# Splitting the second-to-last V load 1/4 and 3/4 around the last K load, with five tiny reads of x in mid-run

## The chip, the cores and the metric

The kernel runs on one core of a Trainium2 chip. The metric is device time in microseconds (us), median of several executions; lower is better. Beside it stands one execution taken by the hardware profiler, with a record of each instruction, each DMA packet and each landing of a load.

Five engines matter here, and each runs its own instructions in program order: PE (TensorE, matmuls; PEld is its weight load), DVE (VectorE), ACT (ScalarE), POOL (GpSimd) and SP (SyncE), which here only issues DMAs. A DMA issued by SP is cut into packets and spread over the core's 16 DMA engines. The load has landed when all 16 have reported.

## The reference

A gated mix of two branches for a single token. Nearly all of the work is branch A: attention of 16 query heads over a cache of 8 key/value heads, 65536 positions and head size 256, in bfloat16.

```python
q = (x @ wq)                                   # 16 heads of 256
k = repeat(k_cache, 2); v = repeat(v_cache, 2) # 8 heads in the cache, 2 query heads for each
p = softmax(einsum("bhqd,bhkd->bhqk", q, k) / 16)
a = einsum("bhqk,bhkd->bhqd", p, v).reshape(1, 1, 4096) @ wo
b = mixer MLP of layernorm(x)                  # w1 1 x 1792, w2 1792 x 1
out = g * a + (1 - g) * b                      # g = sigmoid(sum(x * gate_w))
```

K and V are 8 x 65536 x 256 elements of 2 bytes each, 268 MB apiece. They are read once, and there are two query rows per key head, so the kernel is mostly the reading of 537 MB.

## The kernel before

**Blocks.** The cache is walked in 32 blocks (n = 0 to 31, L = 31 is the last), four per key head. A block is 16384 positions; partition p holds 128 consecutive positions of it, so a block's K, like its V, is 128 partitions x 128 rows x 256 elements, 8.4 MB. K goes into two tiles, kn0 (rows 0 to 63 of each partition) and kn1 (rows 64 to 127); V goes into one tile, vt, of 128 rows. There is one buffer of each, no second set.

**Work in a block.** `score_block(n)` (lines 352 to 364) takes K through 32 quarters (8 groups i of 16 rows, 4 quarters each). A quarter is four PE transposes into PSUM (line 329) and one DVE copy to SBUF (line 334). Each complete group is followed by eight score matmuls (line 343) that accumulate in `sc_ps`. The first 16 quarters read kn0, the other 16 read kn1. `softmax(n)` (line 380) takes the maximum, exponentials and the transposed weights `pT`. `pv(n, ip)` for ip = 0 to 3 (line 366) multiplies the weights with 32 rows of vt each: ip 0 needs rows 0 to 31, ip 1 rows 32 to 63, and so on; it is 16 matmuls (line 370). `accumulate` (line 416) adds the product to the running sum `acc`.

**Order.** `seq` ties every instruction to the one before it on its engine, so the order on each engine is the order of the text. All K and V loads are issued by SP. For most blocks SP issues after the scores of block n: V(n), then the two halves of K(n+1). A load waits until its tile has been read: V(n) for the products of block n-1, K(n+1) into kn0 for the first 16 quarters of block n, into kn1 for the other 16.

**The end.** For block L-1 the order (lines 510 to 514) is: rows 0 to 63 of V(L-1), K(L) into kn0, K(L) into kn1, rows 64 to 127 of V(L-1). The products of block L-1 are put off: two of the four stand within the scores of block L, as hooks at quarters 8 and 14 (line 501), and two stand after the softmax of block L (lines 531 and 532). V(L) isn't loaded into vt but into the two K tiles, in six pieces of 64, 32, 16, 8, 4 and 4 rows (`load_v_last`, line 121): the first into kn0, the other five into kn1. The products of block L (line 552) are another form: 128 rows, two matmuls each, V as the weights, 64 rows from kn0, then the collection of the earlier blocks' sum (`collect`, line 440), then 64 rows from kn1. A short epilogue (lines 560 to 572) scales, projects, copies and stores the output.

**Starting loads.** wq, x and the small vectors are loaded at the start, the small ones from ACT's queue; wo is loaded once in block 0.

Of the kernel before, what the change touches and what calls it, by code (L numbers as in the profile page):

```python
# [9 lines left out]
BF16 = mybir.dt.bfloat16  # L10
# [10 lines left out]
VP = BLK // 128  # L21
KP = VP // 2
NJ = 16
NI = VP // NJ
# [4 lines left out]
def kernel(  # L29
# [15 lines left out]
    nc = tc.nc  # L45
# [12 lines left out]
    def seq(ins):  # L58
        e = ins.ins.engine
        if e in last:  # L60
            tc.add_manual_dep(
                ins.ins,
                last[e],
                mybir.DependencyInfo(
                    mybir.DependencyClass.NoSync, mybir.DependencyReason.DATA
                ),
                reason="program order",
            )
        last[e] = ins.ins.name
        return ins  # L70

    const = ctx.enter_context(tc.tile_pool(name="const", bufs=1))
# [29 lines left out]
    def rows(cache, n):  # L102
        g, b = divmod(n, NB)
        return cache[0, g, b * BLK:(b + 1) * BLK, :].rearrange("(p j) d -> p j d", j=VP)

    def load_k(n, h, pieces=((0, KP),)):
        for j0, j1 in pieces:
            seq(nc.sync.dma_start(
                out=k_tiles[h][:, j0:j1, :],
                in_=rows(A_k_cache, n)[:, h * KP + j0:h * KP + j1, :],  # L110
            ))

    def load_v(n, j0=0, j1=VP):
        seq(nc.sync.dma_start(out=vt[:, j0:j1, :], in_=rows(A_v_cache, n)[:, j0:j1, :]))

    def pairs(ap):
        return ap.rearrange("p (i j) d -> p i j d", i=2)
# [3 lines left out]
    def load_v_last(n):  # L121
        for j0, j1 in LAST:
            seq(nc.sync.dma_start(
                out=k_tiles[j0 // KP][:, j0 % KP:(j1 - 1) % KP + 1, :],
                in_=rows(A_v_cache, n)[:, j0:j1, :],
            ))
# [4 lines left out]
        out=wq_t[:, :], in_=A_wq[DM:D, :].rearrange("r (h n) -> (r h) n", h=2)  # L131
    ))
    with nc.allow_non_contiguous_dma(reason="short rows"):
# [16 lines left out]
        out=val[:], in_=rowsel[:, :, :, 0:NI], op=ALU.add, axis=AXIS.XY  # L150
    ))
    fst = const.tile([128, 2, REP], FP32)
    for e in range(2):
        seq(nc.vector.tensor_reduce(
            out=fst[:, e, :], in_=rowsel[:, :, :, e:e + 1], op=ALU.add, axis=AXIS.XY
# [3 lines left out]
        out=par[:], in_=ident_f[:].rearrange("p (a r) -> p r a", r=REP), op=ALU.add, axis=AXIS.X  # L159
# [3 lines left out]
        out=nval[:], in0=val[:], scalar1=-scale, scalar2=None, op0=ALU.mult  # L163
# [7 lines left out]
        out=same[:], in_=val[:].unsqueeze(1).to_broadcast([128, 64, REP])  # L171
# [10 lines left out]
        out=xrr[:], in_=xr[:, DM:D].unsqueeze(2).to_broadcast([1, D - DM, 2])  # L182
    ))
    x_col = hd_ps[:, 40:44]
    for k in range(3):
# [13 lines left out]
        out=xtm[:], in0=par[:], scalar1=x_col[:, 3:4], scalar2=None, op0=ALU.mult  # L199
# [17 lines left out]
        out=veps[:], in0=mv[:, 1:2], scalar1=1e-5, scalar2=None, op0=ALU.add  # L217
# [5 lines left out]
    for _ in range(2):  # L223
# [3 lines left out]
            out=ntmp[:], in0=ntmp[:], scalar1=-0.5, scalar2=1.5, op0=ALU.mult, op1=ALU.add  # L227
# [3 lines left out]
        out=h_bc[:], in0=xf[:], scalar1=mv[:, 0:1], scalar2=rstd[:, 0:1],  # L231
        op0=ALU.subtract, op1=ALU.mult,
    ))
    for b in range(NF):
        seq(nc.scalar.activation(
            out=gel[:, b, :], in_=h_bc[:], func=ACT.Gelu_apprx_tanh,
# [4 lines left out]
    for h in range(HQ):  # L241
# [19 lines left out]
        out=qpad[:, :, :, 0, 0:REP],  # L261
        in_=q_ps.rearrange("p (c g r) -> p c g r", c=2, r=REP),
    ))
    for i in range(1, NI):
        seq(nc.vector.tensor_copy(
            out=qpad[:, :, :, i, i * REP:(i + 1) * REP], in_=qpad[:, :, :, 0, 0:REP]
# [58 lines left out]
    def transposes(i, quarter):  # L325
        tp = tps[state["t"] % 4]
        state["t"] += 1
        for jj in range(4):
            seq(nc.tensor.transpose(  # L329
                tp[:, jj * 128:(jj + 1) * 128],  # L330
                k_tiles[i // 4][:, i % 4 * NJ + quarter * 4 + jj, :].bitcast(FP32),
                ident_f[:, :],
            ))
        seq(nc.vector.tensor_copy(  # L334
            out=kT_tiles[i % 2][:, quarter * 4:(quarter + 1) * 4, :, :].rearrange(
                "p j n c -> p (j n c)"
            ),
            in_=tp[:, :].bitcast(BF16),
        ))

    def scores(g, i, c):
        for a in range(4):
            seq(nc.tensor.matmul(  # L343
                sc_ps[32 * a:32 * (a + 1), :],
                lhsT=qpad[:, c, g, i, :],
                rhs=kT_tiles[i % 2][:, :, 32 * a:32 * (a + 1), c],
                start=(i == 0 and c == 0),
                stop=(i == NI - 1 and c == 1),
                tile_position=(0, 32 * a),
            ))  # L350

    def score_block(n, hooks={}):
        due = []
        for t, (i, quarter) in enumerate((i, q) for i in range(NI) for q in range(4)):
            transposes(i, quarter)
            if due and due[0][0] <= t:
                scores(n // NB, *due.pop(0)[1])
            if quarter == 3:
                due.append((t + 2, (i, 0)))
                due.append((t + 3, (i, 1)))  # L360
            if t in hooks:
                hooks[t]()
        while due:
            scores(n // NB, *due.pop(0)[1])

    def pv(n, ip):
        pT = pT_tiles[n % 2]
        for jj in range(NJ):
            grp = jj % 4
            seq(nc.tensor.matmul(  # L370
                pv_ps[32 * grp:32 * grp + 2 * REP, :, :],
                lhsT=pT[:, 32 * jj + 2 * REP * ip:32 * jj + 2 * REP * (ip + 1)],
                rhs=pairs(vt[:, 32 * ip:32 * (ip + 1), :])[:, :, jj, :],
                start=(ip == 0 and jj < 4),
                stop=(ip == NI // 2 - 1 and jj >= NJ - 4),
                tile_position=(0, 32 * grp),
            ))
# [38 lines left out]
    def accumulate(n):  # L416
        if n % NB > 0:
            seq(nc.vector.scalar_tensor_tensor(  # L418
                out=acc[:], in0=acc[:], scalar=al_tiles[n % 2][:, 0:1], in1=pv_ps[:, :, :],
                op0=ALU.mult, op1=ALU.add,  # L420
            ))
        else:
            seq(nc.vector.tensor_copy(out=acc[:], in_=pv_ps[:, :, :]))  # L423
# [43 lines left out]
    L = NBLK - 1  # L467

    def products(n):
        for ip in range(NI // 2):  # L470
            pv(n, ip)
        accumulate(n)
# [14 lines left out]
    def last_wo():  # L487
        for r in range(REP):
            for c in range(2):
# [2 lines left out]
                    in_=wo_sb[:, HQ - REP + r, c, :].rearrange("p (m k) -> p k m", k=NCOL),  # L492
                ))

    for n in range(NBLK):
        if n == 0:
            score_block(n, {8: gate_sum, 20: mixer_tail})
        elif n < L:
            score_block(n, {5: gate_column, 16: last_wo} if n == 1 else {})
        else:  # L500
            score_block(n, {4: result_base, 8: lambda: pv(L - 1, 0), 14: lambda: pv(L - 1, 1)})
        if n < L - 1:
            load_v(n)
            load_k(n + 1, 0)
            load_k(n + 1, 1)
            if n == 0:
                seq(nc.sync.dma_start(
                    out=wo_sb[:], in_=A_wo.rearrange("(h p c) n -> p h c n", p=128, c=2)
                ))
        elif n == L - 1:  # L510
            load_v(n, 0, KP)
            load_k(L, 0)
            load_k(L, 1)
            load_v(n, KP, VP)
        else:
            load_v_last(L)
        softmax(n)
        if n == L:
            seq(nc.vector.tensor_scalar(
                out=esc[:], in0=fst[:], scalar1=al_tiles[L % 2][:, 0:1], scalar2=None, op0=ALU.mult  # L520
            ))
            seq(nc.vector.tensor_scalar(
                out=lsv[:], in0=val[:], scalar1=lsum[:, 0:1], scalar2=None, op0=ALU.mult
            ))
            f_ps = tps[0][:, 0:NCOL]
            for k in range(NCOL):
                seq(nc.tensor.matmul(  # L527
                    f_ps[:, k:k + 1], lhsT=base[0:1, k, :],
                    rhs=ones_f[0:1, 0:1], start=(k == 0), stop=False, skip_group_check=True,
                ))  # L530
            pv(n - 1, 2)
            pv(n - 1, 3)
            seq(nc.tensor.matmul(
                hd_ps[:, 456:456 + REP], lhsT=ones_f[:, :], rhs=lsv[:, :], start=True, stop=True
            ))
            accumulate(n - 1)
            seq(nc.vector.reciprocal(out=rdv[:], in_=hd_ps[:, 456:456 + REP]))
            seq(nc.vector.tensor_scalar(
                out=rdv[:], in0=rdv[:], scalar1=gcol[:, 0:1], scalar2=None, op0=ALU.mult
            ))  # L540
        if n < L - 1:
            if n % NB == NB - 1:
                denominators()
            products(n)
            if n % NB == NB - 1:
                head_end(n // NB)


    for j in range(VP):
        i, jj = divmod(j, NJ)  # L550
# [52 lines left out]
```

## Time and profile before

| | |
|---|---|
| Time, median of 3 runs | 1286.46 us (1286.38 to 1286.53) |
| The profiled execution, its own time | 1285.52 us |
| Its span, first to last instruction | 1283.7 us |
| Granted TensorE clock, mean | 0.862 of full speed |
| PE busy | 975.9 us (76%) |
| DVE busy | 756.1 us (59%) |
| ACT busy | 44.9 us (3%) |
| DMA moved | 545.5 MB, mean 425 GB/s |
| Packets under 512 B | 2260 of 17838 |
| K loads of a half block | 63 of 4096 KB, median 26.8 us from issue to landing |
| V loads of a block | 30 of 8192 KB, median 33.6 us from issue to landing |

The shares of busy time are averages over the whole run, in which most of the 32 blocks look alike and the last two don't. The change lies in these last two blocks, but for the tiny reads, so the stretch from about 1195 us to the end is the one to read closely. The times of packets and landings below come from the same profiled execution.

### The profile page before, as it was taken

What the parts mean: (1) busy time and instruction counts of PE and PEld (TensorE: products, weight loads), DVE (VectorE), ACT (ScalarE), POOL (GpSimd) and SP (SyncE); (2) the same over time, 40 slices, a digit from 0 to 9 for tenths busy, and PEclk for the clock granted to TensorE, in tenths of its full rate; (3) what the DMA queues carried; (4) which work ended last, traced back from release to release, by engine and by line L of the source; (5) the groups of instructions that cost most, each with busy time, mean ns of one, the idle gap of its engine ahead of it and who ended that gap; (6) DMA issues with size and microseconds to landing.
All of it is one profiled execution on the core that took longest, in us unless ns stands there. A gap on an engine that the chain in (4) does not pass through costs nothing.

```text
span 1283.7 us, 20141 instructions
## 1 busy us (share of the span) xinstructions
PE 975.9 (76%) x8761; PEld 639.8 (50%) x8761; DVE 756.1 (59%) x1360; ACT 44.9 (3%) x111; POOL 6.3 (0%) x9
## 2 busy tenths in 40 slices
PE   5767777787768888777877788877788767878677
PEld 4444444554445554445554455644455444455455
DVE  6565555665556655556654566645576555676563
ACT  4000000000000000000000000000000000000000
POOL 1000000000000000000000000000000000000000
PEclk9888888988888887888887888878889888898887
DMA  9999999999999999999999999999999999999996
GB/s 409 422 430 428 440 419 433 432 435 434 440 418 435 438 434 430 431 427 434 437 436 438 421 430 434 437 432 431 434 427 436 437 437 423 427 420 438 398 403 255
DMA packets 17838, 545.51 MB, mean 425 GB/s; under 512 B 2260, under 2 KB 4310, under 8 KB 4822
## 3 DMA queue, kind: packets, MB, share of 16 engines
q1 hardware_dynamic: 17312, 544.22, 98.6%
q8 instruction: 68, 1.11, 0.3%
q14 instruction: 20, 0.16, 0.0%
q10 hardware_dynamic: 438, 0.01, 0.0%
HBM read 544.22 MB, written 0.00 MB: 424 GB/s over the span
## 4 chain that ended last, share of the span: by engine, by line
DMA 68%; PE 30%; DVE 2%; issue 0%; DVEq 0%
DMA kn<-in_A_k_cache_dram 67%; PE tps L329 23%; PE sc_ps L343 5%; DVE kT L334 1%; PE pv_ps L370 0%; PE hd_ps L552 0%; PE sm_ps L552 0%; DMA xr<-in_A_x_dram 0%; PE tps L527 0%; PE hd_ps L440 0%; PE sm_ps L440 0%; DVE acc L418 0%; DVE rmax L384 0%; DVE z L278 0%; PE tps L565 0%
## 5 line engine op out<-in xcount | busy, mean ns | idle before, releaser
L334 DVE COPY kT<-tps 128x1024 bf16<-128x1024 bf16 x1024 | 647.1, 685 | 184.2 <-PE tps L329 183.2
L329 PE MATMUL tps<-ident_f,kn 128*128 128x128 f32 x4096 | 603.6, 296 | 108.4 <-DMA kn<-in_A_k_cache_dram 108.4
L329 PEld LDWEIGHTS tps<-ident_f,kn 128*128 128x128 f32 x4096 | 486.8, 151 | 228.8 <-DMA kn<-in_A_k_cache_dram 122.0
L370 PE MATMUL pv_ps<-vt,pT 128*4 128x512 bf16 x1984 | 172.9, 524 | 94.6 <-DMA vt<-in_A_v_cache_dram 90.8
L343 PE MATMUL sc_ps<-kT,qpad 128*32 128x512 bf16 x2048 | 201.0, 393 | 28.2 <-DVE kT L334 28.1
L370 PEld LDWEIGHTS <-pT 128*4 128x4 bf16 x1984 | 58.3, 108 | 195.3 <-issue 132.6
L418 DVE SCALAR_TENSOR_TENSOR acc<-acc,al,pv_ps 128x512 f32<-128x512 f32 x23 | 17.2, 748 | 160.5 <-PE pv_ps L370 160.5
L343 PEld LDWEIGHTS <-qpad 128*32 128x32 bf16 x2048 | 52.9, 93 | 110.8 <-issue 101.7
L400 ACT ACTIVATE p_sb<-sc_ps,nb 128x512 bf16<-128x512 f32 x32 | 22.0, 687 | 1178.4 <-DVE nb L396 1178.4
L423 DVE COPY acc<-pv_ps 128x512 f32<-128x512 f32 x8 | 5.5, 692 | 58.6 <-PE pv_ps L370 58.6
L408 DVE STREAM_TRANSPOSE pT<-p_sb 128x512 bf16<-128x512 bf16 x32 | 22.8, 712 | 28.9 <-ACT p_sb L400 28.9
L384 DVE TENSOR_REDUCE rmax<-sc_ps 128x1 f32<-128x512 f32 x32 | 22.1, 691 | 23.2 <-PE sc_ps L343 23.2
L385 PE MATMUL sm_ps<-ident_f,rmax 128*1 128x128 f32 x32 | 8.8, 276 | 25.4 <-DVE rmax L384 25.4
L393 PE MATMUL sm_ps<-mrun,ones_f 1*128 1x2 f32 x64 | 14.1, 288 | 14.2 <-DVE mrun L392 11.7
L385 PEld LDWEIGHTS sm_ps<-ident_f,rmax 128*1 128x1 f32 x32 | 2.5, 79 | 41.5 <-DVE rmax L384 41.5
L393 PEld LDWEIGHTS sm_ps<-mrun,ones_f 1*128 1x128 f32 x64 | 11.4, 221 | 20.4 <-DVE mrun L392 16.5
L396 DVE CUSTOM_DVE_ANT_0 junk<-sm_ps,nval 128x2 f32<-128x2 f32 x32 | 5.1, 159 | 17.1 <-PE sm_ps L393 17.1
L426 PE MATMUL hd_ps<-lsum,same 128*128 128x1 f32 x14 | 4.1, 362 | 13.9 <-DVE lsum L410 13.9
L426 PEld LDWEIGHTS hd_ps<-lsum,same 128*128 128x128 f32 x14 | 3.5, 311 | 14.5 <-DVE lsum L410 14.5
L386 DVE TENSOR_REDUCE mnew<-sm_ps 1x2 f32<-1x64 f32 x24 | 5.1, 213 | 8.9 <-PE sm_ps L385 8.9
L440 PE MATMUL hd_ps<-esc,acc 128*128 128x2 f32 x32 | 5.4, 274 | 6.0 <-DVE acc L418 6.0
L440 PEld LDWEIGHTS hd_ps<-esc,acc 128*128 128x128 f32 x32 | 4.8, 211 | 9.6 <-DVE acc L418 9.6
(99 smaller groups left out, 138.0 us busy)
## 6 DMA issues: line engine op xcount, KB each, us to landing
kn<-in_A_k_cache_dram SPq DMA_DIRECT2D x63, 4096.0 KB, 26.8
vt<-in_A_v_cache_dram SPq DMA_DIRECT2D x2, 4096.0 KB, 27.4
kn<-in_A_k_cache_dram SPq DMA_DIRECT2D x2, 2048.0 KB, 11.7
kn<-in_A_v_cache_dram SPq DMA_DIRECT2D x1, 4096.0 KB, 14.2
wo_sb<-in_A_wo_dram SPq DMA_DIRECT2D x1, 3584.0 KB
vt<-in_A_wq_dram SPq DMA_DIRECT2D x1, 3072.0 KB, 10.4
kn<-in_A_v_cache_dram SPq DMA_DIRECT2D x1, 2048.0 KB, 13.6
kn<-in_A_v_cache_dram SPq DMA_DIRECT2D x1, 1024.0 KB, 13.4
```

The costliest lines, as they stand in the source:

```text
L329: seq(nc.tensor.transpose(tp[:, jj * 128:(jj + 1) * 128], k_tiles[i // 4][:, i % 4 * NJ + quarter * 4 + jj, :].bitcast(FP32), ident_f[:, :],))
L334: seq(nc.vector.tensor_copy(out=kT_tiles[i % 2][:, quarter * 4:(quarter + 1) * 4, :, :].rearrange("p j n c -> p (j n c)"), in_=tp[:, :].bi ...
L343: seq(nc.tensor.matmul(sc_ps[32 * a:32 * (a + 1), :], lhsT=qpad[:, c, g, i, :], rhs=kT_tiles[i % 2][:, :, 32 * a:32 * (a + 1), c], start=( ...
L370: seq(nc.tensor.matmul(pv_ps[32 * grp:32 * grp + 2 * REP, :, :], lhsT=pT[:, 32 * jj + 2 * REP * ip:32 * jj + 2 * REP * (ip + 1)], rhs=pair ...
L384: seq(nc.vector.tensor_reduce(out=rmax[:], in_=sc_ps[:, :], op=ALU.max, axis=AXIS.X))
L385: seq(nc.tensor.transpose(sm_ps[0:1, 0:128], rmax[:, 0:1], ident_f[:, :]))
L393: seq(nc.tensor.matmul(sm_ps[:, 128:128 + REP], lhsT=ones_f[0:1, :], rhs=mrun[0:1, :], start=True, stop=True))
L400: seq(nc.scalar.activation(out=p_sb[:, :], in_=sc_ps[:, :], func=ACT.Exp, scale=scale, bias=nb[:, 0:1], accum_out=den[:, 0:1],))
L408: seq(nc.vector.transpose(out=pT[:, :], in_=p_sb[:, :]))
L418: seq(nc.vector.scalar_tensor_tensor(out=acc[:], in0=acc[:], scalar=al_tiles[n % 2][:, 0:1], in1=pv_ps[:, :, :], op0=ALU.mult, op1=ALU.add,))
L426: seq(nc.tensor.matmul(hd_ps[:, 460:461], lhsT=same[:].rearrange("p a r -> p (a r)"), rhs=lsum[:, 0:1], start=True, stop=True,))
L440: seq(nc.tensor.matmul(o_ps[c], lhsT=acc[:, e, :].rearrange("p (d c) -> p c d", c=2)[:, c, :], rhs=weights[:, e, :], start=(start and e == ...
```

## The change

The V load of block L-1 is cut at row 32 and not at row 64: 32 rows ahead of the two halves of K(L), 96 rows behind them. The product over rows 32 to 63 (ip = 1) of block L-1 is no longer a hook at quarter 14 of block L; it stands after the softmax of block L, in front of the two that were there. In five blocks (n = 20, 22, 24, 26 and 28) SP also issues, between V(n) and K(n+1), a read of the first k elements of x, one element of 2 bytes to each of k partitions, k = 1, 2, 4, 8 and 12, each into its own column of a new small tile that nothing reads.

```diff
+    COUNTS = {20: 1, 22: 2, 24: 4, 26: 8, 28: 12}
+    some = const.tile([16, len(COUNTS)], BF16)
+
+    def rows_read(n, k):
+        i = sorted(COUNTS).index(n)
+        with nc.allow_non_contiguous_dma(reason="short rows"):
+            seq(nc.sync.dma_start(
+                out=some[0:k, i:i + 1], in_=A_x[0, 0, 0:k].rearrange("(p o) -> p o", o=1)
+            ))
+
     for n in range(NBLK):
...
         else:
-            score_block(n, {4: result_base, 8: lambda: pv(L - 1, 0), 14: lambda: pv(L - 1, 1)})
+            score_block(n, {4: result_base, 8: lambda: pv(L - 1, 0)})
         if n < L - 1:
             load_v(n)
+            if n in COUNTS:
+                rows_read(n, COUNTS[n])
             load_k(n + 1, 0)
             load_k(n + 1, 1)
...
         elif n == L - 1:
-            load_v(n, 0, KP)
+            load_v(n, 0, 32)
             load_k(L, 0)
             load_k(L, 1)
-            load_v(n, KP, VP)
+            load_v(n, 32, VP)
...
-            pv(n - 1, 2)
-            pv(n - 1, 3)
+            for ip in range(1, NI // 2):
+                pv(n - 1, ip)
```

KP is 64, VP is 128 and NI is 8.

## The prediction

> **What bounds the kernel now.** I read the page first: the row of DMA and GB/s slices, then the chain.
>
> ```profile
> span 1283.7 us, 20141 instructions
> ...
> DMA  9999999999999999999999999999999999999996
> GB/s 409 422 430 428 440 419 433 432 435 434 440 418 435 438 434 430 431 427 434 437 436 438 421 430 434 437 432 431 434 427 436 437 437 423 427 420 438 398 403 255
> ...
> DMA 68%; PE 30%; DVE 2%; issue 0%; DVEq 0%
> ```
>
> The reader is to see that the load stream is full for 37 of 40 slices, so that until about 1190 us only bytes count, and the change moves the same bytes. The last three slices are thinner (398, 403, 255): what can be won lies there. So next the chain of waits in order of time, from 1204 us on:
>
> ```profile
> 1215.87 19.33 DMA kn<-in_A_k_cache_dram
> 1235.25 5.38 PE tps L329 x24
> ...
> 1243.06 0.97 PE pv_ps L370 x16
> ...
> 1248.57 0.86 PE pv_ps L370 x16
> ...
> 1260.89 0.70 DVE kT L334
> ...
> 1265.26 3.35 PE pv_ps L370 x32
> 1268.63 0.75 DVE acc L418
> 1272.92 0.85 PE hd_ps L440 x4
> 1273.78 0.85 PE sm_ps L440 x4
> ```
>
> No load stands in it after K(L) lands in kn0 at 1235.20. From there to the end it is PE: scores of block L, both products left from L-1, the products of L. Did the data wait for PE, or PE for the data? The table of stretches for the instructions that touch kn, whose columns are stretch, its length, PE and PEld busy (count), granted clock, DMA share, GB/s:
>
> ```profile
> 1269.40:1273.00 3.60, 3.41 (x128) 3.32 (x127) 0.81 0.64 252
> 1273.00:1274.66 1.66, 0.17 (x7) 0.38 (x8) 0.50 0.04 15
> 1274.66:1278.10 3.44, 3.38 (x127) 3.29 (x124) 0.50 0.02 5
> ```
>
> In the last 3.4 us PE is full and DMA moves nothing (5 GB/s is one instruction fetch). The loads of V(L) give the same: the last 4 rows are issued at 1260.88 and land 13.4 us later, at 1274.31, while PE ends the products at 1278.06. So the end of the kernel hangs on the PE chain that starts with the landing of K(L), and 3.7 us behind the last byte.
>
> **Why that landing is late, and what the 16 engines do.** The landing marks (one per DMA engine and load) show the engines apart: of V(L-2) the first engine is done at 1183.78 and the last at 1195.58. Seven are early, nine late; the late ones carry the PE instruction fetches (68 of 16 KB, 0.9 us each). A load counts as landed with the last engine. Through the tail that engine is never out of work: its marks stand at 1195.58, 1205.24, 1235.20, 1254.52, 1264.20 and 1269.05, which is 9.7 us for each 4 MB, with 0.9 more for a fetch before 1235.20. The early engines do run dry:
>
> ```profile
> 1208.00:1212.00 4.00, 3.61 (x34) 2.44 (x32) 3.79 (x7) 0.00 (x0) 0.00 (x0) 1.00 0.93 401
> 1212.00:1216.00 4.00, 4.00 (x37) 2.84 (x36) 3.55 (x7) 0.00 (x0) 0.00 (x0) 1.00 0.63 270
> 1216.00:1220.00 4.00, 4.00 (x38) 2.81 (x37) 3.77 (x7) 0.00 (x0) 0.00 (x0) 1.00 0.99 410
> ```
>
> (PE, PEld, DVE, ACT, POOL, clock, DMA share, GB/s.) The 0.63 is the early engines out of work until K(L) is issued at 1215.87, which costs nothing, because they aren't last.
>
> **The change, part by part.**
>
> 1. *32 rows of V(L-1) fewer ahead of K(L).* That is 2 MB, half of 9.7, 4.85 us of the last engine. K(L) into kn0 lands at 1235.20 - 4.85 = 1230.35, if SP has issued it by then. SP issues it when the quarters of block L-1 on kn0 are through, at 1215.87 as now. From issue to the first byte is 1.8 us (the first mark, 1227.36, less 9.70, is 1217.66), and the last engine comes free from the shorter piece at 1230.35 - 9.70 - 0.9, about 1219.8: 2.1 us of cover. For kn1: issued 1226.70, ready 1228.5, wanted 1230.35, 1.85 us of cover. Without cover, each us dry is a us later for all data behind it. The early engines run dry for 9.6 and not 4.7 us; they have the time.
>
> 2. *96 rows behind K(L).* The last engine's bytes up to there are the same, so V(L-1) ends at 1254.5 and the last byte of V(L) at 1274.3, as now. V(L) into kn0 waits for quarter 16 of block L, which comes earlier. So the end of the data doesn't move: it is the floor.
>
> 3. *PE from 1230.35.* PE is idle from 1230.0, so it starts at once. The scores now take 1260.89 - 1235.25 = 25.64 us to the last copy; the hook that is gone was 0.86 to 0.97, which leaves 24.7. The first 24 transposes ran cold (0.50 clock, 5.38 us, where 12 warm ones with their scores stand at 0.68 a quarter: 4.1); with no gap ahead of them up to 1.2 us of this goes too, of which I count half, 0.6. Last copy at 1230.35 + 24.1 = 1254.5. From it to the first product of L are 8.62 us now (1260.89 to 1269.51), and the third product of L-1 behind the softmax adds 16 x 0.105 (3.35 us for 32) = 1.68: 1264.8. The V rows it wants landed at 1254.5, so it doesn't wait. The gain on the chain so far is 1269.51 - 1264.8 = 4.7.
>
> 4. *Products of L against the floor.* 128 matmuls take 3.4 us, the collection 1.7: rows 64 on could start at 1269.9 (landed 1269.05), and would be done by 1273.3; but rows 112 on land at 1273.0, 1273.7 and 1274.31. So the last four rows decide: 1274.31, plus 0.05 to start (as at 1235.20 to 1235.25), 8 matmuls at 0.027 = 0.21, and 0.14 for the last one: 1274.7. Before: 1278.06. **Gain 3.35 us**; the 1.35 left over of the 4.7 is lost waiting for data.
>
> 5. *The epilogue* (1278.06 to 1283.7) is unchanged.
>
> 6. *Tiny reads.* SP issues them right behind V(n), where it then waits for PE some 11 to 16 us (V(28) issued 1122.94, K(29) 1137.39); an issue takes 0.33 to 0.5, so SP is covered, and nothing reads the tile. On the DMA engines: 1 + 2 + 4 + 8 + 12 = 27 packets of 2 B and five marks. The packet records show 4-byte marks and 28-byte pieces at 9 ns, and a mark pushing its engine's next packet back 12 to 14 ns. Were all 32 on the last engine: 0.4 us; none on it: 0. No tiny read on SP's queue is in the trace, so the far bound is the whole round trip of the nearest small transfer, the output store: issued 1279.06, landed 1282.80, 3.74 us, five times 18.7. I take 0.1, by the rows for packets of the same size.
>
> The Trainium skill speaks against this part ("DMA: Bandwidth & Descriptors", Specifications and Rules for kernel authors): below 512 B an engine does a read-modify-write, and transfers under 64 KB are mostly overhead, with about 2.0 us fixed for a DMA in its fit; as an estimate from that page, five in a row on one engine would be 10 us. The same page (Why a DMA increments its semaphore by 16 and not by 1) has such a DMA run on the lowest-numbered engines, so one engine would be in all five; no row here numbers the engines. The 9 ns packets say that this overhead is latency, not engine time; if the page's 2.0 were engine time on the last engine, the sum would be 6.6 us slower.
>
> **Sum.** 1283.7 - 3.35 + 0.1 = 1280.4 of span; the profiled execution's own 1285.52 becomes 1282.3. It stands 0.94 under the median of the runs, so the time is 1286.46 - 3.25 = **1283.2**. A measurement here tells 0.2% (2.6 us) from no change: the forecast is 0.25%, just beyond it. Its own range is 1282.3 (a fetch of 0.9 no longer on the last engine) to 1284.1 (one more on it).
>
> **Rivals.**
>
> A. *The end moves less than 2.6 us.* PE has only 1.2 us to spare in step 4 (it could begin the products at up to 1266, by 1274.3 less 3.4, 1.7 and 3.2), and the loads 1.85 to 2.1. For: both covers are small. Against: the warm start was only half counted. A stretch of 1.3 us without work on the last engine, or one more fetch and 0.4 us, takes the gain to 2.0: time 1284.5 with the tiny reads.
>
> B. *K(L) doesn't come earlier, so the split does nothing.* If K(L) were held by its issue and not by the bytes ahead, PE would start at 1235.2 as now, with 1.68 - 0.97 = 0.7 more behind the softmax: 1287.2. For: the early engines do wait for that issue. Against: the last one doesn't (9.7 us per 4 MB without a hole).
>
> C. *The other side: a tiny read holds its engine for its round trip.* Place: the last engine, five times, each 3.74 us: 18.7 - 3.35, time 1301.8. It decides from 0.67 us a read (five eat the gain), and is measurably slower from 1.2. For: nothing in the trace shows one amid bulk loads on this queue. Against: the 9 ns packets, and if the engine is an early one, it has up to 11.8 us of lead to lose first.
>
> **How the numbers follow.** Forecast 0.62, A 0.24, B 0.06, C 0.08. Faster by over 0.2% is the forecast's 0.62. Within 0.2% are A and B, 0.30. Slower is C, 0.08. The range starts at 1281.8 (0.5 below the forecast's own, for the other half of the warm start and PE's pace) and reaches over A to 1286.4, no change; it leaves out B, C and a little of the forecast.
>
> **What would show it.** Right: K(L) lands at kn0 near 1230.4; PE idle shrinks there from 5.2 us to under 1; the products of L start near 1264.8, and some of their last matmuls wait for a DMA; the stretch of full PE without DMA at the end is gone. Wrong: landing marks of the last engine with holes after 1215 (A), an unmoved K(L) (B), a landing of V or K behind a tiny read that is later by microseconds than its neighbours (C). The marks of the tiny reads themselves, on 1, 2, 4, 8 and 12 partitions, tell which engines are early and which late.

## The result, and the profile after

The change made the kernel slower: 1289.41 us median (1288.76 to 1290.4, 8 runs) beside 1286.03 (1285.29 to 1286.53, 8 runs), a ratio of 1.0028, 95% interval 1.0017 to 1.0039, or 3.4 us. The forecast was 1283.2 with a range up to 1286.4.

The profiled execution after took 1289.28 us. From its page, the slices and the chain:

```profile
span 1287.5 us, 20146 instructions
...
DMA  9999999999999999999999999999999999999897
GB/s 406 423 433 422 432 421 434 427 441 427 438 421 428 442 432 425 425 433 427 443 428 436 423 428 431 436 432 424 428 433 428 439 418 430 425 430 432 349 408 313
...
DMA 68%; PE 29%; DVE 2%; issue 0%; DVEq 0%
DMA kn<-in_A_k_cache_dram 67%; PE tps L329 24%; PE sc_ps L343 5%; DVE kT L334 2%; DMA kn<-in_A_v_cache_dram 2%; DMA xr<-in_A_x_dram 0%; PE pv_ps L370 0%; DVE rmax L384 0%; DVE z L278 0%; PE sm_ps L393 0%; PE tps L577 0%; DVE zt L277 0%; PE sm_ps L475 0%; PE sm_ps L385 0%; PE hd_ps L564 0%
```

Against the page of before there is a load of V(L) in the chain (`kn<-in_A_v_cache_dram`), which wasn't there: the end now waits for data, as was forecast. The chain in order of time, its last pieces (start, us, what; the products of L are line 564 now):

```profile
1261.79 19.61 DMA kn<-in_A_v_cache_dram
1281.40 0.05 issue
1281.45 0.19 PE hd_ps L564
...
1281.84 0.16 DVE oT L573
```

PE ends 0.44 us behind the last landing (1281.40 to 1281.84), where it was 3.75 (1274.31 to 1278.06). That part came as worked out: 3.3 us. But the last landing itself is 7.1 us later.

Where that begins is seen by asking both traces when PE starts on a block's K. First the kernel before, PE in the stretch around block 16, in the middle of the run (start us, us, instructions, and in brackets what it waited for):

```profile
657.52 4.25 PE L329 MATMUL tps<-ident_f,kn 128*128 128x128 f32 x23 [1.85 <-DMA kn<-in_A_k_cache_dram]
```

The same of the kernel after:

```profile
660.89 0.88 PE L329 MATMUL tps<-ident_f,kn 128*128 128x128 f32 x6 [0.98 <-DMA kn<-in_A_k_cache_dram]
```

PE waits for the same load in both, and after it is 3.37 us late, at a time when the first tiny read (issued at 814.49) and the changed loads of the last blocks are still to come. The lag grows evenly: 0.46 us at block 1, 1.89 at 8, 3.37 at 16, 4.84 at 24, 5.68 at 30, which is some 0.18 us a block. From block 30 to the last landing 1.4 us more are added. But for the tiny reads, the instructions of these blocks are the same in both kernels, so the loads themselves are the place to look. The packet records say by how much (ns, packets of the loads on SP's queue):

```
                     10%    median   75%    90%    mean
before  32 KB       1213    1213    1213   1213   1217.4
after   32 KB       1213    1216    1221   1224   1221.6
before  64 KB       2418    2418    2418   2418   2427.5
after   64 KB       2418    2421    2426   2428   2434.9
```

A DMA engine moves 16 of the 32 KB and 8 of the 64 KB in a block: 16 x 4.2 + 8 x 7.4 = 126 ns of the 180. The rest isn't in the lengths of the packets, and where it is was not found.

What can make every packet longer from the first block on? The change has one thing that is there from the start: the new tile. In the pool `const` it is the last, behind it come K, V and all the work tiles. The memory plan of the program shows 10 bytes rounded up to 32, and everything behind moved by that:

```
tile          before     after     (byte in each partition)
some             -       69632
kn0           69632      69664
kn1          102400     102432
vt           135168     135200
kT0          200704     200736
```

### The profile page after: what moved, and what is told of

The parts are those of the page before. It is cut to its first block, busy times and chain, and to the rows that moved or that the text cites. A ratio compares the mean times of both kernels' runs of the same rounds, so it can differ in the third digit from the quotient of the medians.

```text
span 1287.5 us, 20146 instructions
## 1 busy us (share of the span) xinstructions
PE 970.5 (75%) x8761; PEld 636.4 (49%) x8761; DVE 755.2 (59%) x1360; ACT 44.9 (3%) x111; POOL 6.3 (0%) x9
## 4 chain that ended last, share of the span: by engine, by line
DMA 68%; PE 29%; DVE 2%; issue 0%; DVEq 0%
DMA kn<-in_A_k_cache_dram 67%; PE tps L329 24%; PE sc_ps L343 5%; DVE kT L334 2%; DMA kn<-in_A_v_cache_dram 2%; DMA xr<-in_A_x_dram 0%; PE pv_ps L370 0%; DVE rmax L384 0%; DVE z L278 0%; PE sm_ps L393 0%; PE tps L577 0%; DVE zt L277 0%; PE sm_ps L475 0%; PE sm_ps L385 0%; PE hd_ps L564 0%
## 5 line engine op out<-in xcount | busy, mean ns | idle before, releaser
L393 PE MATMUL sm_ps<-mrun,ones_f 1*128 1x2 f32 x64 | 13.5, 279 | 14.1 <-DVE mrun L392 11.7
```

The source lines that it names most:

```text
L393: seq(nc.tensor.matmul(sm_ps[:, 128:128 + REP], lhsT=ones_f[0:1, :], rhs=mrun[0:1, :], start=True, stop=True))
```

## Experiments

Theory P is that this place of the tiles costs the time; R that the tiny reads do; S that the split does. In the indented texts, which were written before each run, a ring that runs dry is a DMA engine without work. Each run was measured beside the kernel before on the same chip.

**1. The split alone.** No reads and no tile for them.

```diff
-            load_v(n, 0, KP)
+            load_v(n, 0, 32)
...
-            load_v(n, KP, VP)
+            load_v(n, 32, VP)
```

(with the moved product as in the change)

> The split of the V load and the moved product alone: no tiny reads and no tile for them. Theory P (place: the 10-byte tile pushes the K and V tiles from byte 69632 of a partition to 69664, and every load packet is slower for it from the first block on): the K and V tiles stand where they stood, so the 3.3 us of the split are won, 1282.7 beside 1286.0, last K half landing near 1230.4. Theory R (the tiny reads slow the DMA engines): the same 1282.7. Theory S (the split itself is dear, by rings run dry): 1288 to 1289.5.

Measured: 1284.41 beside 1285.69, ratio 0.9987 (0.9979 to 0.9996). Faster, so S falls; but by 1.3 us and not by 3.3.

**2. The reads alone**, their tile at the end of the last pool.

```diff
+    some = work.tile([16, len(COUNTS)], BF16)
...
+            if n in COUNTS:
+                rows_read(n, COUNTS[n])
```

> The five tiny reads alone, their tile at the end of the last pool, so that no other tile moves; V split in halves as before. Theory P: 1286.0, no change within 0.4 us. Theory R: 1288.9 to 1292, all of the 3.4 us that were lost and up to the 3.3 us that the split should have won. Theory S: 1286.0.

Measured: 1285.57 beside 1285.69, ratio 0.9998 (0.9989 to 1.0007). The reads cost nothing that can be measured; R falls.

**3. The tile alone**, in the place that it has in the change.

```diff
     gcol = const.tile([128, 1], FP32)
+    pad = const.tile([16, 5], BF16)
+    seq(nc.gpsimd.memset(pad[:], 0.0))
```

> The kernel before with nothing but a 10-byte tile (set to zero once at the start) in the place of the change's tile, so that the K and V tiles stand 32 bytes further on; no reads, no split. Theory P: 0.18 us more in each block from the first on, 5.7 us by block 30 and about 6.5 at the end: 1291.5 to 1293. Theories R and S: 1286.0.

Measured: 1291.64 beside 1285.69, ratio 1.0046 (1.0033 to 1.0058): 5.95 us for ten bytes that nobody reads. PE around block 16 in this kernel (its lines are two further down):

```profile
660.76 1.12 PE L331 MATMUL tps<-ident_f,kn 128*128 128x128 f32 x4 [0.25 <-DMA kn<-in_A_k_cache_dram]
```

It starts 3.24 us later than before, nearly as in the changed kernel (3.37), and the packets have the same lengths (1213, 1216, 1221, 1224 ns).

**4. The whole change with its tile moved to the end.**

```diff
-    some = const.tile([16, len(COUNTS)], BF16)
+    some = work.tile([16, len(COUNTS)], BF16)
```

> The whole change, but with the tile for the tiny reads at the end of the last pool, so that the K and V tiles stand where they stood before. Theory P: 1282.8, faster by 3.2. Theory R: 1289.4, as the change. Theory S: 1289.4 as well.

Measured: 1283.1 beside 1285.69, ratio 0.998 (0.9972 to 0.9989). One word turns the change from 3.4 us slower into 2.6 us faster. P stands.

**5 to 7. How far must the tiles be moved to be right again?** The pad of experiment 3 with 64, 128 and 256 bytes.

```diff
+    pad = const.tile([16, 32], BF16)     # 64 bytes; 64 and 128 elements in the others
```

> The kernel before with an unused tile of 64 bytes a partition ahead of the K and V tiles, which then start at byte 69696. The 32-byte shift cost 5.9 us. Theory 64 (a load is slower when its tile does not start on 64 bytes): 1285.7, as before. Theory 256 (it has to start on 256 bytes): 1291.6. Theory far (a larger boundary, of a row of 512 bytes or of the 4096 on which the tiles stand before): 1291.6.

> The same with 128 bytes. Theory 64: 1285.7. Theory 256: 1291.6. Theory far: 1291.6.

> The same with 256 bytes. Theory 64: 1285.7. Theory 256: 1285.7. Theory far: 1291.6.

| Shift, bytes | us | ratio, interval | 90% of the 32 KB packets, ns |
|---|---|---|---|
| 32 | 1291.64 | 1.0046 (1.0033 to 1.0058) | 1224 |
| 64 | 1290.63 | 1.0038 (1.0023 to 1.0053) | 1222 |
| 128 | 1290.47 | 1.0036 (1.0023 to 1.0049) | 1221 |
| 256 | 1285.72 | 1.0000 (0.9991 to 1.0010) | 1213 |

With 256 the start of block 16 is back as well:

```profile
657.75 3.96 PE L331 MATMUL tps<-ident_f,kn 128*128 128x128 f32 x19 [1.63 <-DMA kn<-in_A_k_cache_dram]
```

Theory 64 and theory far fall: it is the 256 bytes. The Trainium skill has a rule that bears on this ("DMA: Bandwidth & Descriptors", How a descriptor splits into AXI transactions): a descriptor is cut into transactions of 256 B, which begin on a 256-byte boundary, so one that starts elsewhere takes in unused bytes ahead of its start (the page's example of 576 B takes four transactions and not three). The boundary agrees with the runs (1213 ns at 256 bytes, 1221 to 1224 at 32, 64 and 128). Two things don't come out of the page: it speaks of the bytes that are fetched, and here the source stayed where it was while the destination moved; and it counts the unused bytes ahead of the start, by which 128 should be dearer than 32, while the runs show 4.7 us beside 5.95 (with intervals that overlap) and packets of 1221 ns beside 1224. That extra transactions are the cause was not shown; the boundary was. Whether it is the destination by itself that counts, or where it stands against the source, isn't told apart either, because the source was never moved.

**8. Only the work tiles moved**, K and V where they were.

```diff
+    pad = work.tile([16, 5], BF16, name="pad")
     kT_tiles = [work.tile([128, NJ, 128, 2], BF16, name=f"kT{i}") for i in range(2)]
```

> The kernel before with a 10-byte tile behind the K and V tiles and ahead of the work tiles: kT, p_sb, pT and all later ones move by 32 bytes, K and V do not. If the loads' own destination is what counts: 1285.7 and 32 KB packets of 1213 ns at the 90th percentile. If a shift of what PE and DVE read and write counts: 1291.6.

Measured: 1285.69 beside 1285.78, ratio 0.9998 (0.9989 to 1.0008), packets at 1213 ns. So it is the destination of the loads that counts, not where PE and DVE work.

**9 to 11. Why the split wins less than was worked out.** In the trace of experiment 1 K(L) landed at 1230.89, near the 1230.35 of the forecast, but the last landing stood at 1275.49, 1.2 us later than before. Theory cover says that DMA engines run out of work ahead of K(L); theory bytes, which is the forecast's, that the end of the data is fixed. Two other cuts, and the first once more.

```diff
-            load_v(n, 0, 32)
+            load_v(n, 0, 48)        # and 48 to VP; in the other 16 and 16 to VP
```

In the cut at 16 the first product can't stand within the scores either, and all four come behind the softmax.

> V of the second-to-last block cut at row 48 (no tiny reads, no tile), the second product behind the softmax as in the change. K lands 2.4 us earlier than before and not 4.85. Theory cover (at 32 rows the DMA engines are out of work before both halves of K, some 0.6 us each time for the first packet and the wait for the issue on top, and the end of the data moves back by 1.2 to 1.8): with 48 rows the last engine has 2.4 us more of work, the data end where they did before (1274.3 in the trace), and PE sets the end, 1.7 us earlier than before: 1284.0. Theory bytes (the end of the data is fixed and only the landing of K counts): 1284.0 as well, but then 32 rows must be better than this by 1.6 us.

> Cut at row 16, all four products of the second-to-last block behind the softmax. Theory cover: the ring is dry by 2.4 us more ahead of K, all data behind it are as much later, the last landing near 1278: 1286.5 to 1287, no better than before. Theory bytes: the end of the data stays at 1274.3 to 1275.5 and PE is early enough: 1282.5 to 1284.

> The split at 32 rows alone once more, beside the other two on one chip; it gave 1284.4 and the whole change with its tile moved away 1283.1. Theory cover: 1283 to 1284.5, the spread coming from when PE frees the K tile. Theory bytes: 1282.4 and better than the cut at 48 rows by 1.6.

Measured: 48 rows 1283.66, ratio 0.9984 (0.9975 to 0.9992); 16 rows 1286.55, ratio 1.0003 (0.9995 to 1.0012); 32 rows again 1283.35, ratio 0.9984 (0.9975 to 0.9993), beside 1285.85. The cut at 16 is what theory cover said and theory bytes excluded; 48 is as good as 32, not worse by 1.6. The repeat lies in cover's 1283 to 1284.5; bytes had 1282.4.

The traces show where the work runs out. In the cut at 16, stretches of 4 us (length, PE, PEld, DVE, ACT, POOL, clock, DMA share, GB/s):

```profile
1212.00:1216.00 4.00, 4.00 (x40) 3.19 (x36) 3.55 (x6) 0.00 (x0) 0.00 (x0) 1.00 0.36 152
1216.00:1220.00 4.00, 4.00 (x39) 2.56 (x37) 3.78 (x8) 0.00 (x0) 0.00 (x0) 1.00 0.46 135
1220.00:1224.00 4.00, 4.00 (x39) 3.07 (x36) 3.56 (x7) 0.00 (x0) 0.00 (x0) 1.00 0.90 389
```

PE is full and the load stream at 0.36 and 0.46: K(L) isn't issued until 1218.12, because PE hasn't freed its tile. The tile is free when PE has done 16 quarters of block L-1, and how long these take goes with the granted clock at their start. In the repeat of the cut at 32 (the columns are the same):

```profile
1205.30:1209.30 4.00, 3.54 (x31) 3.08 (x32) 3.24 (x6) 0.00 (x0) 0.00 (x0) 1.00 0.78 336
```

and in experiment 4, where the stretch is the first 4 us of the block too:

```profile
1205.00:1209.00 4.00, 3.92 (x19) 3.92 (x20) 2.29 (x4) 0.00 (x0) 0.00 (x0) 0.50 0.82 352
```

At a clock of 1.00 PE gets through 31 transposes and score matmuls in these 4 us, at 0.50 through 19. The kernel before has both within one trace. From PE's start on a block's K to the next issue into kn0 it took 10.6 us in blocks 24, 28 and 30, whose first 4 us stood at a clock of 1.00, and 11.7 to 11.8 in blocks 25, 26, 27 and 29, where the clock was 0.57 to 0.65.

The table gives the time from the landing of K(L-1) to the issue of K(L), from that landing to the last of V(L) (traces, us), and how many of the 16 DMA engines still had a packet of 8 KB or more under way just ahead of K(L)'s first:

| Kernel | rows ahead of K(L) | K(L-1) to issue of K(L) | K(L-1) to last landing | engines at work |
|---|---|---|---|---|
| before | 64 | 10.6 | 69.1 | 9 |
| reads only | 64 | 11.8 | 69.0 | 9 |
| 256-byte shift | 64 | 12.8 | 68.9 | 9 |
| cut at 48 | 48 | 11.8 | 69.2 | 9 |
| cut at 32, repeat | 32 | 10.6 | 69.2 | 8 |
| cut at 32, experiment 1 | 32 | 11.8 | 70.1 | 1 |
| change as it stands | 32 | 11.8 | 70.5 | 1 |
| change, wider tile (experiment 12) | 32 | 11.6 | 71.0 | 1 |
| change, tile at the end | 32 | 12.7 | 71.1 | 1 |
| cut at 16 | 16 | 12.9 | 73.8 | 0 |

With 64 or 48 rows ahead the late issue costs nothing. With 32 a late issue leaves one engine of 16 at work, and the end of the data is 1 to 2 us later; not in step with the issue, though (11.6 goes with 71.0, 11.8 with 70.1). With 16 it is 4.7 us later. At 32 rows it isn't the last engine that runs dry. In experiment 1 that one reported the 32 rows of V at 1219.84 and went straight on into K(L); the others had begun K(L) at 1218.1 to 1219.1 from nothing, and the mark that ends K(L), 1230.89, is that of one of these, which then met an instruction fetch of 0.96 us. An engine that starts again from nothing also has a first packet that is some 0.6 us longer (in experiment 4 fifteen of 32 KB that start from 1218.7 to 1219.1 exceed 1213 ns by 0.46 to 0.75). The table is of single executions; that the clock is what moves them was not tried by itself.

In the repeat, where PE was quick, the trace is close to the forecast's. It is the fastest of its eleven executions (1282.68; the slowest took 1285.9). The end of its chain:

```profile
1253.78 20.77 DMA kn<-in_A_v_cache_dram
1274.55 0.05 issue
1274.60 0.18 PE hd_ps L552
...
1274.99 0.16 DVE oT L561
```

K(L) landed at 1230.00 (1230.35 forecast), the last landing stood at 1274.55 (1274.3), PE ended at 1274.99 (1274.7), and this execution took 1282.68 (1282.3). The products began at 1264.54 (1264.8), but that agreement is luck: PE had waited 1.87 us for the first piece of V(L) by then.

**12. The change with a wider tile**, at the place that it has.

```diff
-    some = const.tile([16, len(COUNTS)], BF16)
+    some = const.tile([16, 128], BF16)
```

> The whole change as it stands, tile in the same pool and at the same place, but 256 bytes wide in each partition and not 10, so that the K and V tiles start at byte 69888. Theory 256 (only the start of the load's tiles on 256 bytes counts, and the rest of the change wins 1.3 to 2.6): 1283.0 to 1284.4, and 32 KB packets of 1213 ns at the 90th percentile. If anything else in the change were dear: 1286 to 1289.4.

Measured: 1283.9 beside 1285.65, ratio 0.9984 (0.9975 to 0.9993), 32 KB packets at 1213 ns. Nothing else in the change is dear. This version, the one with the tile at the end (1283.1) and the cuts alone at 32 and 48 rows beat both kernels by 1.3 to 2.6 us; the intervals don't tell them from each other.

## Why the prediction was wrong

**The sum.** 5.95 us for the place of the tiles (experiment 3), less 1.3 to 2.6 won by the split (experiments 1, 4, 11 and 12), and nothing that can be told from zero for the reads (experiment 2): 3.4 to 4.7 slower, measured 3.4.

**The step that failed** is step 6, and with it the opening sentence that the change moves the same bytes. It priced the five reads and their packets, and the tile only as something that "nothing reads". That a tile which is laid ahead of K and V moves them, and that the loads' rate hangs on where they stand, had no term, no bound and no rival; it measured 5.95 us. The slices of the page could not have shown it: before, the K and V tiles stood on 256 bytes, and no row has another place. But the tile's pool and its place behind the others are in the diff, and the question what stands behind it would have led to a bound. The load stream is full for 37 of 40 slices, so a slowdown of every load by 0.46% has nothing to hide behind: that is 6 of 1286 us.

**Steps 1 and 2, the size.** The mechanism held: K(L) earlier, PE earlier, the data as the floor. But of the 3.35 us the split won 1.3 to 2.6. The cover of 2.1 and 1.85 us was taken from one block, in which the 16 quarters took 10.6 us. The same trace has 10.6 in only 4 of its 31 blocks; the others took 11.0 to 13.3, with a median of 11.7 over all. With that the cover of the last engine is between 2 us and nothing. It was also reckoned for that engine alone: the other eight late ones had reported the 64 rows at 1222.20 to 1223.18, 1.4 to 2.4 us ahead of its 1224.56, so that by the same working they had 0.7 us of cover or none. The sentence that the engines which run dry "have the time" thus failed for the rest of the late ones, and the end of the data isn't fixed but moves back by 0.1 to 2 us. In the trace of before block L-1 began at a clock of 1.00 and block L at 0.50; the forecast counted the cold clock as a gain to come for block L, and not as a risk for block L-1. In the changed kernel all this was to be seen too:

```profile
1212.00:1216.00 4.00, 4.00 (x24) 3.44 (x23) 3.52 (x6) 0.00 (x0) 0.00 (x0) 0.58 0.66 283
1216.00:1220.00 4.00, 4.00 (x38) 2.81 (x37) 3.34 (x6) 0.00 (x0) 0.00 (x0) 1.00 0.51 217
1220.00:1224.00 4.00, 4.00 (x38) 2.81 (x37) 3.75 (x7) 0.00 (x0) 0.00 (x0) 1.00 0.60 205
```

A clock of 0.58 at the start of block L-1, and loads at half rate until K(L) is issued. SP's own rows in the changed kernel:

```profile
1203.18 0.33 SPq L114 DMA_DIRECT2D vt<-in_A_v_cache_dram  x1
1222.72 11.15 SPq L108 DMA_DIRECT2D kn<-in_A_k_cache_dram  x2
1233.93 0.43 SPq L114 DMA_DIRECT2D vt<-in_A_v_cache_dram  x1
```

Between the quarter of V at 1203.18 and K(L) at 1222.72 nothing is issued for 19.5 us; before it was 16.6 (1199.25 to 1215.87) with twice the rows ahead.

**Steps 4 and 5 were right, step 3 in its direction.** PE ended 0.44 us behind the last landing in both the change and the repeat of the cut at 32; the forecast had 0.4 (1274.31 to 1274.7). In the repeat step 3 was too slow: the last copy came at 1253.79 and not 1254.5, and the three products behind the softmax took 4.45 us and not 5.0. It cost nothing, because the data were the floor.

**The reads, step 6 proper, were right.** Their 27 packets took 9 ns each. A mark pushes the next packet of its engine back by 6 ns and not 12 to 14: without one that packet starts 4 ns ahead of the end of the one before, with one 2 ns behind it. That only makes the term smaller. The estimate that the fixed 2.0 us for a DMA would give, 10 us, isn't in the runs: 1285.57 beside 1285.69. The 2.0 us is the Trainium skill's fit for DMAs issued from GpSimd ("DMA: Bandwidth & Descriptors", Anatomy of one DMA — SWDGE (gpsimd) path), while these are issued from SP.

**The rivals.** A's time is that of the split in experiment 1, where the tiles stand right (1284.41 beside 1284.5). Its mechanism holds in part: engines were without work, but not the last one. B was wrong: K(L) came earlier by 3.7 to 5.2 us wherever the tiles stood right and the cut was at 32. C was wrong: the reads landed right behind their own V load (on four partitions 1004.44, V's last mark 1004.25). The slower side had been given to the reads alone, and what made the kernel slower was the declaration of their tile.

## What to carry to other kernels

A new tile can have a price even if nothing uses it: see what is laid out behind it, and keep the tiles that bulk loads write on multiples of 256 bytes in each partition, which is one word or some padding. When a kernel runs at the rate of its loads, look at the packet lengths of the whole run before looking for the cause in the stage that was changed. And a cover that is read off one block is only as good as the clock in it: give it the slowest time that the same work has anywhere in the trace, and reckon it for every DMA engine and not for the last alone.

## What the runs showed of the hardware that was not expected

The tiny reads on SP's queue tell something of the order of the DMA engines. Of a V load seven engines report early and nine late, 8 to 11 us apart by 1000 us. The read on one partition landed early, on two both early, on four three early and one last of all (993.14, 993.23, 993.31 and 1004.44 us, where V's own marks run from 992.95 to 1004.25), on eight five early, on twelve six early. This fits a wider read that uses the engines of the narrower ones and some more, as the Trainium skill has it ("DMA: Bandwidth & Descriptors", Why a DMA increments its semaphore by 16 and not by 1: the lowest-numbered engines). The engine that ends every load is then the third or the fourth: it isn't in the reads on one and two partitions, and its mark is the last in those on four, eight and twelve.

The loads' rate was the same to 1 ns in most packets of 32 KB as long as the tiles stood on 256 bytes (1213 at 10%, 50%, 75% and 90%), and spread over up to 11 ns as soon as they didn't.
